# Seven block products in place of a plain output product for the first two token blocks, and quads of whole weights

## The chip, the cores and the metric

The kernel runs on one core of one Trainium2 chip. TensorE (PE) multiplies matrices into PSUM, VectorE (DVE), ScalarE (ACT) and GpSimd (POOL) work on elements, SyncE (SP) issues most transfers. The metric is the device time of one execution in microseconds, the median of three runs.

## The reference, cut to what matters

Three layers in float32: a chunked attention, a gated layer and a layer with a rational activation. The change is in the gated layer (its output product) and in the attention's softmax.

```python
# attention: 4 batches, 8 heads, 768 positions, head size 64, chunks of 32 queries,
# each against 8 memory keys and a window of 56 keys: 64 keys a chunk
a = exp(scores - max(scores));  a = a / (sum(a) + 1e-9);  out = a @ v_full
# gated layer: 3072 tokens, 512 -> 1536 -> 512
x = (sigmoid(x @ w_gate) * (x @ w_val)) @ w_out
# third layer: 512 -> 2048 -> 512
h = x @ w_in
P = a[0] + a[1]*h + a[2]*h**2 + a[3]*h**3
Q = 1 + abs(b[0])*abs(h) + abs(b[1])*h**2
y = (P / (Q + 1e-6)) @ w_out2
```

## The kernel before

**Products.** Each float32 operand is split into a rounded part (`hi`, written by ScalarE) and a remainder (`lo`, by VectorE), and each product is three matmuls (`TERMS`: hi·hi, hi·lo, lo·hi) of 128x128 weights on 512 tokens. Weights come as 64-bit words; `conv_scale` (two ScalarE instructions) and `conv_bits` (one on VectorE) turn 512 columns of them into float32.

**Blocks.** The 3072 tokens are six blocks of 512. Blocks 0 and 1 go through 24 steps `(j, f)`, one for each block j and each of twelve weight slices f of 128 inner columns. A step multiplies gate and value (`gate_val`, 24 matmuls into tiles `h`), forms sigmoid times value, splits it (`g_split`) and runs the output product of the step before (`out1`, 12 matmuls into four banks `acc`). Attention tiles for later blocks (`attn_*` for one tile of 128 tokens, `pair_*` for two), weight conversion, and combinations of weights for later are laid between, by step number, with `at(step, function, ...)`.

**Block products.** Blocks 2 to 5 are taken as two pairs. For a pair of blocks `ja, ja + 1` and a pair of slices `fp`, gate and value are seven products of sums and differences of block operands (`PRODUCTS`, function `quad`), each of 12 matmuls, run as two halves `m` (gate, value) of 6 matmuls a product. Weights of kind "a" are loaded already split (`wqa`, 512 KB), those of kind "s" (sums, `wqs`, 256 KB) are loaded whole and split. The result is held in tiles `gh` by names "11", "21", "12", "22" (slice even or odd, first or second block). The output product of a pair is then seven block products too (`OUTS`), over three groups k of four slices: 21 visits `(i, k)` of 12 matmuls (`out_step`, or `early` for the three that lie among the quads). Before a visit its operand is formed by differences (`o_pre`), split (`o_split`, 1024 wide, tiles `oh` and `ol`) and its weights are loaded (`o_weights`).

**Third layer.** Blocks 0 to 5 in three pairs, by products `q_X`, `q_Y`, `q_Z` and an output product into `acc`; the text of this part is not touched.

**Order.** All operations are recorded, and a planner (`Recorder.plan`) orders them before they are issued. TensorE keeps the order of recording. For the others it simulates the engines with estimated costs, takes the task with the earliest due time (`late`), and not much earlier than that (`window`), if the buffers that it needs are free. Each engine then runs its list in order, waiting on semaphores. Every recorded instruction has line L485, so tiles tell them apart; a tile's name is that of the buffer's last naming.

**Buffers.** Pools `w` (20 of 4 KB a partition), `x` (4) and `b` (8) of 8 KB, `g` (4), `t` (7, used as 14 halves), and PSUM pools `acc` (4 banks) and `ps` (4 banks).

Of the kernel before, what the change touches and what calls it, by code (L numbers as in the profile page):

```python
# [11 lines left out]
F32 = mybir.dt.float32  # L12
# [30 lines left out]
AHEAD = 3  # L43
# [148 lines left out]
class Recorder:  # L192
# [13 lines left out]
    def cost(self, t, op, args, kw):  # L206
# [107 lines left out]
    ORDERED = "gwxb"  # L314
    DMA_WINDOW, CAP, DMA_CAP, STORE_CAP, RATE = 12.0, 12.0, 12.0, 14.0, 350e3

    def plan(self):
# [45 lines left out]
        events = []  # L363
        self.stalls = []
        while left:
# [3 lines left out]
            for e in engines:  # L369
# [46 lines left out]
                used = now if t.table else used  # L416
                if t.table and t.table != table:
                    table, extra = t.table, 1.29
# [70 lines left out]
def fused_kernel(ctx: ExitStack, tc: tile.TileContext, q, k, v, w1, w2, coef, x2d, w2o, wq2, wqa, wqs, wqo, out):  # L489
# [100 lines left out]
    BYSET = (1, 3)  # L590

# [25 lines left out]
    def attn_exp(t):  # L617
        s = s_sb[t]
        if t not in BYSET:
# [3 lines left out]
        r = rs[t] = spool.tile([P, NSET, 1], F32, tag="r", name=f"r{t}")  # L623
        sps = sc_ps.pop(t, None)
        for h in range(2):
            for i in range(4):
# [63 lines left out]

    def pair_qk(t):
# [19 lines left out]

    def pair_max(t):
# [4 lines left out]
        if edge(t) or edge(t + 1):  # L717
# [4 lines left out]
            else:  # L722
# [5 lines left out]
        mv = m.rearrange("p (a h) w -> p a h w", h=2)  # L728
        for h in range(2):
# [76 lines left out]
    def unit1(f, u):  # L806
        if u == 2:
            if ("o", f) not in wf:
                wf["o", f] = t2(f"wfo{f}")
            return wf["o", f]  # L810
# [26 lines left out]
    def split_out_hi(key, src):  # L837
        t = split_tile(key)
        nc.scalar.activation(out=halves(t, 0), in_=src.rearrange("p (m c) -> p m c", m=2), func=ACTF.Copy)

# [1385 lines left out]
```

## Time and profile before

| | |
|---|---|
| median of three runs | 1119.76 us (1119.12 to 1121.26) |
| the profiled execution | 1118.92 us |
| its span in the trace | 1117.1 us |
| TensorE busy | 1104.8 us, 99% of the span |
| VectorE busy | 954.3 us, 85% |
| ScalarE busy | 777.7 us, 70% |
| transfers | 303.05 MB |

The span runs from the first to the last profiled instruction; the time of an execution also holds what lies around it. Busy times are unions of instructions; as instructions overlap, one instruction's own duration is longer than the time it adds.

### The profile page before, as it was taken

The page shows a single profiled execution, that of the slowest core. Times are in us where ns is not written, and L with a number is a line of the kernel's source. Part 1 is how long each engine was busy: PE and PEld are TensorE (multiplying, and loading weights), DVE is VectorE, ACT ScalarE, POOL GpSimd, SP SyncE. Part 2 cuts the span into 40 slices and gives each one's busy share as a digit, 9 for nine tenths or more (in the row PEclk, how much of TensorE's full clock was granted, in tenths as well). Part 3 has the DMA queues.
Part 4 walks back from the last instruction along what each step waited for, and adds up shares of the span by engine and source line. Part 5 has one row for each costly group of instructions (what it writes and reads, how often), then busy time and mean ns, then how long its engine had stood idle before and what let it go on. Part 6 is the DMA issues. An engine that isn't in the chain of part 4 may idle for free.

```text
span 1117.1 us, 20117 instructions
## 1 busy us (share of the span) xinstructions
PE 1104.8 (99%) x7743; PEld 905.7 (81%) x7743; DVE 954.3 (85%) x1284; ACT 777.7 (70%) x1159; POOL 23.1 (2%) x39
## 2 busy tenths in 40 slices
PE   8999999999999999999999999999999999999998
PEld 4888888888888788888878888888888887888887
DVE  4798868887899898799889799999889989999992
ACT  5999555665566675565375798875898874998952
POOL 0000000000000000000000000000000000000000
PEclk8999999999999999999999999999999999999999
DMA  9899869988877887798948687789577888687682
GB/s 369 311 352 363 317 243 385 324 306 308 310 243 275 307 309 247 276 367 309 329 146 294 191 268 206 226 292 318 170 234 211 235 295 292 197 255 207 219 248 93
DMA packets 111167, 303.05 MB, mean 271 GB/s; under 512 B 10848, under 2 KB 11104, under 8 KB 111072
## 3 DMA queue, kind: packets, MB, share of 16 engines
q1 hardware_dynamic: 107040, 287.78, 73.6%
q0 software_dynamic: 3456, 12.58, 6.2%
q8 instruction: 61, 1.00, 0.4%
q10 hardware_dynamic: 576, 1.41, 0.3%
q14 instruction: 34, 0.28, 0.1%
HBM read 225.18 MB, written 63.96 MB: 259 GB/s over the span
## 4 chain that ended last, share of the span: by engine, by line
PE 84%; issue 12%; DVE 1%; DMA 1%; ACT 1%; POOL 0%; POOLq 0%; ACTq 0%
PE acc L485 22%; PE p L485 19%; PE h L485 12%; PE q_X L485 9%; PE ob_X L485 6%; PE q_Z L485 4%; PE ob_Z L485 3%; PE xp L485 2%; PE q_Y L485 2%; PE sp L485 2%; PE ob_Y L485 2%; PE tp L485 1%; DMA q<-u 1%; PE idle L485 1%; DMA k<-k_in 0%
## 5 line engine op out<-in xcount | busy, mean ns | idle before, releaser
L485 PE MATMUL acc<-w2o,G 128*128 128x512 f32 x1152 | 268.4, 389 | 0.0
L485 PEld LDWEIGHTS acc<-w2o,G 128*128 128x128 f32 x1152 | 216.2, 188 | 44.9
L485 PE MATMUL q_X<-x,wi 128*128 128x512 f32 x576 | 146.4, 389 | 0.7 <-ACT hA L485 0.7
L485 PE MATMUL p<-b,wpq_s 128*128 128x512 f32 x576 | 138.6, 389 | 0.0
L485 PE MATMUL h<-x,wp 128*128 128x512 f32 x576 | 137.5, 392 | 0.0
L485 PEld LDWEIGHTS q_X<-x,wi 128*128 128x128 f32 x576 | 108.0, 188 | 23.7 <-ACT hA L485 1.1
L485 PEld LDWEIGHTS p<-b,wpq_s 128*128 128x128 f32 x576 | 108.0, 188 | 22.7 <-issue 0.3
L485 PEld LDWEIGHTS h<-x,wp 128*128 128x128 f32 x576 | 107.4, 188 | 22.4
L485 ACT ACTIVATE st<-st 128x512 f32<-128x512 f32 (+1 forms) x124 | 77.1, 667 | 8.5 <-DMA st<-w_in 8.4
L485 PE MATMUL p<-x,wpq_a 128*128 128x512 f32 x288 | 73.6, 391 | 0.0
L485 PE MATMUL q_Z<-x,wi 128*128 128x512 f32 x288 | 73.1, 389 | 0.0
L485 PE MATMUL acc<-g,wp 128*128 128x512 f32 x288 | 72.1, 394 | 0.0
L485 PEld LDWEIGHTS q_Z<-x,wi 128*128 128x128 f32 x288 | 54.1, 188 | 11.2
L485 PEld LDWEIGHTS p<-x,wpq_a 128*128 128x128 f32 x288 | 53.7, 188 | 11.4
L485 PE MATMUL ob_X<-oh,ow 128*128 128x512 f32 x192 | 62.3, 392 | 0.3 <-ACT oh L485 0.3
L485 PEld LDWEIGHTS acc<-g,wp 128*128 128x128 f32 x288 | 53.1, 188 | 11.5
L485 ACT ACTIVATE u<-q,qc 128x1024 f32<-128x1024 f32 x48 | 54.9, 1146 | 10.3 <-DMA q<-u 9.4
L485 DVE SCALAR_TENSOR_TENSOR q<-q,u 128x1024 f32<-128x1024 f32 x48 | 58.2, 1219 | 4.1 <-ACT u L485 4.1
L485 DVE SCALAR_TENSOR_TENSOR t<-t,cf,u 128x1024 f32<-128x1024 f32 x48 | 61.2, 1278 | 0.0
L485 ACT ACTIVATE u<-u 128x1024 f32<-128x1024 f32 (+1 forms) x57 | 55.9, 988 | 5.4 <-DVE u L485 4.9
L485 ACT ACTIVATE hb<-q_X 128x512 f32<-128x512 f32 x48 | 28.4, 591 | 38.6 <-PE q_X L485 38.5
L485 ACT ACTIVATE G<-hb 128x512 fp32r<-128x512 f32 x48 | 29.9, 626 | 31.4 <-PE acc L485 27.7
(355 smaller groups left out, 2007.5 us busy)
## 6 DMA issues: line engine op xcount, KB each, us to landing
w2o<-w2o SPq DMA_DIRECT2D x96, 512.0 KB, 4.9
wi<-wq SPq DMA_DIRECT2D x72, 512.0 KB, 4.8
st<-w_in SPq DMA_DIRECT2D x62, 512.0 KB, 6.2
ow<-wqo SPq DMA_DIRECT2D x42, 512.0 KB, 6.2
wpq_a<-wqa SPq DMA_DIRECT2D x36, 512.0 KB, 5.9
v<-v_in SPq DMA_DIRECT2D x24, 512.0 KB, 5.7
wpq_s<-wqs SPq DMA_DIRECT2D x48, 256.0 KB, 5.8
q<-u POOLq DMA_DIRECT2D x24, 512.0 KB, 6.0
```

Source lines behind the costliest of these rows:

```text
L485: getattr(getattr(self.nc, t.eng), op)(*[real(x) for x in args], **{n: real(x) for n, x in kw.items()})
```

## The change

- The output product of blocks 0 and 1 is no longer made step by step (`out1`, `g_split`, `store1` go). Sigmoid times value of all 24 steps is held in `gh` tiles, and the product is made as seven block products like that of the other pairs: six visits (i of 0 and 1) in steps 14 to 23 with weights that stay in SBUF (`"o1"`, `"o2"`), and 15 visits after the steps (`outs(0, O0, STEPS0)`).
- Output weights are loaded and converted apart (`load_wo`, `conv_wo`) from step 8 on; the sums of gate and value weights (`w_comb`) come from step 3 on in place of step 10.
- The gate and value weights that the quads read are stored and loaded whole (256 KB), and split after the load.
- A quad takes both halves m of a product before the next product, in another order of products, over banks X and Y of two halves each. Loads run five products ahead.
- The softmaxes of pairs 8, 10, 12 and 14 are taken set by set: exponential with the maximum as bias and a running sum, for each of 16 sets of 64 keys. Pair 20 is copied out of PSUM first.
- Pairs 8 to 14, eight second-layer weights and the combinations of tokens move to other steps; the planner lets stores to DRAM go up to 30 us ahead, and holds a change of activation table back only while tasks of the loaded table remain.

```diff
-AHEAD = 3
+AHEAD = 5
...
-            t.window = self.DMA_WINDOW
+            t.window = self.STORE_WINDOW if out.cell.row == 1 << 60 else self.DMA_WINDOW
...
+    STORE_WINDOW = 30.0
...
-                        if t.table and table and t.table != table and now > used + 1.5 and t.late > now - stall + 4:
+                        if t.table and tables.get(table) and t.table != table and now > used + 1.5 and t.late > now - stall + 4:
...
+    SETS = (8, 10, 12, 14)
...
-        if t not in BYSET:
+        if t not in BYSET + SETS:
...
-        r = rs[t] = spool.tile([P, NSET, 1], F32, tag="r", name=f"r{t}")
+        n = NSET if t < NPAIR else 2 * NSET
+        r = rs[t] = spool.tile([P, n, 1], F32, tag="r", name=f"r{t}")
...
+    COPIED = (20,)
...
+        if t in SETS:
+            for h in range(2):
+                nc.vector.tensor_reduce(out=mv[:, :, h, 0], in_=sps[h], axis=AX.X, op=ALU.max)
+            sc_ps[t] = sps
+            set_shift(t, m)
...
-        r = spool.tile([P, 2 * NSET, 1], F32, tag="r", name=f"r{t}")
-        nc.vector.tensor_reduce(out=r[:, :, 0], in_=s, axis=AX.X, op=ALU.add)
+        if t not in SETS:
+            r = rs[t] = spool.tile([P, 2 * NSET, 1], F32, tag="r", name=f"r{t}")
+            nc.vector.tensor_reduce(out=r[:, :, 0], in_=s, axis=AX.X, op=ALU.add)
+        r = rs.pop(t)
...
-        tiles = [None] * 3
+        tiles = [None] * 2
         if 0 < f < 3:
-            pair = [bpool.tile([P, 2, 512], I64, tag="b", name=f"stp{f}_{i}") for i in range(2)]
-            tiles = [pair[0][:, 0], pair[0][:, 1], pair[1][:, 0]]
-        for u in range(3):
+            pair = bpool.tile([P, 2, 512], I64, tag="b", name=f"stp{f}")
+            tiles = [pair[:, 0], pair[:, 1]]
+        for u in range(2):
             load_stage(f"1_{f}_{u}", w1[:, f, u * 512 : (u + 1) * 512], tiles[u])
...
+    def load_wo(f):
+        load_stage(f"o_{f}", w1[:, f, 1024:1536])
+
+    def conv_wo(f):
+        conv_scale(f"o_{f}")
+        t = so[f] = t2(f"so{f}")
+        conv_bits(f"o_{f}", t)
...
-            nc.vector.tensor_tensor(out=sg, in0=sg, in1=pt, op=ALU.mult)
+            o = f"{1 + f % 2}{1 + j}"
+            nc.vector.tensor_tensor(out=g_held(0, o, f // 2), in0=sgs.pop((j, f)), in1=pt, op=ALU.mult)
...
-        (("a", 0, 0), "11", 0),
-        (("s", 1), "2", 1),
-        (("s", 0), "1", 2),
-        (("s", 2), "3", 3),
-        (("a", 0, 1), "21", 0),
-        (("s", 3), "22", 2),
-        (("a", 1, 1), "4", 3),
+        (("a", 0, 0), "11", "X"),
+        (("a", 0, 1), "21", "Y"),
+        (("s", 1), "2", "X"),
+        (("s", 2), "3", "Y"),
+        (("s", 0), "1", "X"),
+        (("a", 1, 1), "4", "Y"),
+        (("s", 3), "22", "X"),
...
-            key = quad_key(ja, fp, w)
-            if w[0] == "a":
-                load_split(key, wqa[2 * fp + w[1], w[2]])
-                continue
-            t = split_tile(key)
+            t = split_tile(quad_key(ja, fp, w))
             hi, lo = t[:, 0], t[:, 1]
-            nc.sync.dma_start(out=lo.bitcast(F32), in_=wqs[4 * fp + w[1]])
+            src = wqa[fp, w[1] + w[2]] if w[0] == "a" else wqs[4 * fp + w[1]]
...
-    def quad(ja, fp, m, fill):
+    def quad(ja, fp, visit):
...
+            if i < 2:
+                for m in range(2):
+                    bank[n, m] = ps(f"p{ja}_{fp}_{m}_{n}")
+            wt, x = wp.pop(quad_key(ja, fp, w)), xop[ja, o]
+            for m in range(2):
+                for kt in range(2):
+                    c = m * 256 + kt * P
+                    for t, (a, b) in enumerate(TERMS):
+                        nc.tensor.matmul(
+                            bank[n, m],
+                            lhsT=wt[:, a, c : c + P],
+                            rhs=x[:, kt, b],
+                            start=(i in (0, 1, 3) and kt == 0 and t == 0),
+                            stop=(kt == 1 and t == 2),
+                            skip_group_check=True,
+                        )
+            if i + AHEAD < len(PRODUCTS):
+                quad_load(ja, fp, i + AHEAD, 1)
+            elif fp < NF1 // 2 - 1:
+                quad_load(ja, fp + 1, i + AHEAD - len(PRODUCTS), 1)
+
+        def copy(name, n):
+            t = [t2(f"{name}_{ja}_{fp}_{m}") for m in range(2)]
+            for m in range(2):
+                nc.scalar.activation(out=t[m], in_=bank[n, m], func=ACTF.Copy)
+            return t
+
+        def add(t, n):
+            for m in range(2):
+                nc.vector.tensor_tensor(out=t[m], in0=t[m], in1=bank[n, m], op=ALU.add)
 
...
+            if c is None:
+                sg, y = t2(f"sg{j}_{f}"), bank["X", 1]
+                nc.scalar.activation(out=sg, in_=bank["X", 0], func=ACTF.Sigmoid)
+            else:
+                sg, y = c
+                nc.scalar.activation(out=sg, in_=sg, func=ACTF.Sigmoid)
...
         product(0)
-        u = t2(f"u_{tag}")
-        nc.scalar.activation(out=u, in_=bank[0], func=ACTF.Copy)
+        h = copy("h", "X")
         product(1)
-        add(u, u, bank[1])
+        add(h, "Y")
+        done(ja, f0, h)
         product(2)
-        v = t2(f"v_{tag}")
-        add(v, u, bank[2])
+        u = copy("u", "X")
+        visit()
         product(3)
-        add(v, v, bank[3])
-        done(jb, f1, v)
+        z = copy("z", "Y")
         product(4)
-        done(ja, f0, None)
-        fill()
+        add(z, "X")
+        done(jb, f1, z)
         product(5)
-        c12 = t2(f"c12_{tag}")
-        add(c12, u, bank[2])
-        done(jb, f0, c12)
+        add(u, "Y")
+        done(ja, f1, u)
         product(6)
-        add(u, u, bank[3])
-        done(ja, f1, u)
+        done(jb, f0, None)
...
-    HELD_B = {2: ("12", "11"), 4: ()}
+    HELD_B = {0: ("11", "21"), 2: (), 4: ()}
...
-    def out1(j, f, mid=None):
...
+        if ja == 0 and i < 2:
+            ow[ja, i, k] = [flat(wp[f"o{1 + i}", 2 * k + f])[:, 0:512] for f in range(2)]
+            return
...
+    def early(ja, i, k):
+        o_weights(ja, i, k)
+        o_split(ja, i, k)
+        o_mm(ja, i, k)
...
+    def w1_store(fp):
+        t = wf["gv", fp]
+        nc.sync.dma_start(out=wqa[fp, 0:2].rearrange("u p n -> p u n"), in_=t[:, 0])
+        nc.sync.dma_start(out=wqa[fp, 2], in_=t[:, 1, 1])
...
+    def o_split1(fp):
+        split_out(("o1", fp), so[2 * fp], 1)
+        split_out(("o2", fp), so[2 * fp + 1])
...
+    def o_store1(fp):
+        nc.sync.dma_start(out=wqo[fp, 0], in_=flat(wp["o1", fp])[:, 0:512].bitcast(F32))
+        store_split(("o2", fp), out_slots(fp, 2))
...
-        s0 = 10 + i // 2
+        s0 = 2 * (i // 4) + 3 + i % 4 // 2
...
+    for fp in range(NF1 // 2):
+        s0 = 8 + 2 * fp
+        for f in (2 * fp, 2 * fp + 1):
+            at(s0, load_wo, f)
+            at(s0 + 1, conv_wo, f)
+        at(s0 + 1, o_split1, fp)
+        at(s0 + 2, o_store1, fp)
+        at(s0 + 2, o_comb, fp)
+        at(s0 + 3, o_store, fp)
+    EARLY0 = ((14, 0, 0), (16, 1, 0), (18, 0, 1), (19, 1, 1), (21, 0, 2), (23, 1, 2))
+    for si, i, n in EARLY0:
+        at(si, early, 0, i, n)
+    for n in range(3):
+        at(max(EARLY0[2 * n][0] + 1, 12 + 4 * n + 3), o_pre, 0, n, "13")
+    STEPS0 = [(i, n) for i in range(2, len(OUTS)) for n in range(NF1 // 4)]
...
-    for t, s0, s1 in ((8, 9, 14), (10, 12, 17), (12, 15, 20), (14, 18, 22)):
+    O0 = len(steps)
+    S1 = O0 + len(STEPS0)
+    for t, s0, s1 in ((8, 13, 18), (10, 16, 21), (12, 19, O0 + 1), (14, 22, O0 + 5)):
...
+    combs(2, [(O0 + i, o, 0) for i, o in zip((2, 3, 5, 8, 10), ("1", "2", "3", "22", "4"))])
+    combs(2, [(O0 + i, o, 1) for i, o in zip((6, 7, 8, 10, 12), ("1", "2", "3", "22", "4"))])
+    at(S1 - 3, quad_load, 2, 0, 0, AHEAD)
...
-    conv_out = [4, 5, 7, 17, 19, 20, 22, S1] + [S1 + i for i in range(5, 12)] + [Q2 + 8]
+    conv_out = [S1, S1 + 1, S1 + 2, S1 + 3] + [S1 + i for i in range(5, 12)] + [O1 + i for i in (6, 9, 12, 15)] + [Q2 + 8]
...
-            g_split((1, j, f), sgs.pop((j, f)), 512)
             run(attn_qk, attn_max, conv2_hi, conv2, x_comb_hi)
-            run(o_whole, o_comb)
-            if si:
-                out1(*steps[si - 1], mid=lambda: run(pair_out, pair_qk, pair_max))
+            run(conv_wo, o_split1, o_comb)
+            run(pair_out, pair_qk, pair_max)
             run(pair_sum)
+            run(o_pre)
+            run(early)
             run(x_comb_lo, conv2_lo, conv2_bits, comb2)
             run(done2)
 
...
+        outs(0, O0, STEPS0)
...
-            wqa = dp.tile([NF1, 2, P, 2, 512], F32, name="wqa")
+            wqa = dp.tile([NF1 // 2, 3, P, 512], F32, name="wqa")
```

Edits left out here: the names of the moved calls in the step loop and in `quads` (which now calls `quad` once per pair of slices, with the second half's side work in `visit`), the first weights' conversions at the start, where those of the output weights go, and the deleted bodies of `out1`, `g_split`, `store1` and `o_whole`.

## Rows read from the trace of the kernel before

**Rows 1.** The page: busy us of each engine, and TensorE's clock in 40 slices.

```profile
PE 1104.8 (99%) x7743; PEld 905.7 (81%) x7743; DVE 954.3 (85%) x1284; ACT 777.7 (70%) x1159; POOL 23.1 (2%) x39
...
PEclk8999999999999999999999999999999999999999
```

**Rows 2.** Chain that ended last: start us, us, what.

```profile
41.50 2.72 PE acc L485 x12
44.22 5.44 PE h L485 x24
...
424.53 8.16 PE ob_X L485 x36
...
449.01 57.12 PE p L485 x252
```

**Rows 3.** TensorE's timeline at both ends of quads: start us, us, instruction, idle before.

```profile
388.38 0.50 PE L485 MATMUL ob_X<-ol,ow 128*128 128x512 f32 x1 [1.18 <-DVE ol L485]
...
571.67 0.49 PE L485 MATMUL ob_X<-oh,ow 128*128 128x512 f32 x1 [0.25 <-ACT oh L485]
573.17 0.50 PE L485 MATMUL ob_X<-ol,ow 128*128 128x512 f32 x1 [1.01 <-DVE ol L485]
```

**Rows 4.** Windows: length, busy us of PE, PEld, DVE, ACT, POOL, then clock, DMA share, GB/s.

```profile
40.00:60.00 20.00, 20.00 (x209) 16.14 (x208) 17.45 (x30) 19.97 (x37) 0.00 (x0) 1.00 0.93 313
...
30.62:138.55 107.93, 107.93 (x1077) 87.91 (x1077) 90.64 (x160) 94.67 (x169) 0.34 (x2) 1.00 0.95 337
138.55:254.09 115.54, 115.54 (x1361) 95.69 (x1361) 90.11 (x152) 67.17 (x113) 0.34 (x2) 1.00 0.86 314
254.09:387.20 133.11, 133.11 (x1073) 109.37 (x1072) 114.62 (x171) 77.34 (x121) 0.49 (x3) 1.00 0.82 292
388.38:449.01 60.63, 60.63 (x752) 50.63 (x753) 51.22 (x64) 40.18 (x62) 0.00 (x0) 1.00 0.76 261
...
573.17:606.18 33.01, 33.00 (x144) 27.03 (x145) 32.44 (x44) 23.46 (x33) 0.00 (x0) 1.00 0.77 254
```

**Rows 5.** Groups of instructions, shapes apart, TensorE: busy us, mean ns of one.

```profile
L485 PE MATMUL acc<-g,wp 128*128 128x512 f32 x288 | 72.1, 394 | 0.0
```

**Rows 6.** VectorE's timeline near 386 us.

```profile
385.37 0.69 DVE L485 TENSOR_TENSOR gh<-v,c 128x512 f32<-128x512 f32 x1
385.98 1.22 DVE L485 TENSOR_TENSOR ot<-gh,gh 128x1024 f32<-128x1024 f32 x1
387.11 1.22 DVE L485 TENSOR_TENSOR ol<-gh,oh 128x1024 fp32r<-128x1024 f32 x1
```

**Rows 7.** ScalarE's timeline near 388 us.

```profile
387.54 0.63 ACT L485 ACTIVATE wpw<-c 128x512 fp32r<-128x512 f32 x1
388.06 1.78 ACT L485 ACTIVATE st<-st 128x512 int32<-128x512 uint32 x3
```

**Rows 8.** Groups of instructions, shapes apart, ScalarE.

```profile
L485 ACT ACT_TABLE_LOAD x25 | 32.1, 1283 | 10.6 <-DMA wqs<-sf 5.7 <-PE h L485 2.2 <-issue 2.2
...
L485 ACT ACTIVATE s<-s 128x1024 f32<-128x1024 f32 x8 | 8.5, 1061 | 0.1
```

**Rows 9.** ScalarE's timeline in a softmax taken set by set.

```profile
10.44 0.31 ACT L485 ACTIVATE s<-sp,m 128x64 f32<-128x64 f32 x1
10.64 0.20 ACT L485 ACTIVATION_READ_ACCUMULATOR s<-sp,m 128x1 f32 x1
10.73 0.32 ACT L485 ACTIVATE s<-sp,m 128x64 f32<-128x64 f32 x1
```

**Rows 10.** Transfers by issue: count, KB each, median us to landing.

```profile
wpq_a<-wqa SPq DMA_DIRECT2D x36, 512.0 KB, 5.9
```

**Rows 11.** Waits of SyncE's queue: us in total, times, longest.

```profile
SPq L485 <- PE acc L485: 108.6, 43, 9.1
```

**Rows 12.** TensorE's timeline at the start.

```profile
27.07 0.54 PE L485 MATMUL xp<-at,v 64*64 64x32 f32 x22 [0.49 <-issue]
...
30.27 3.98 PE L485 MATMUL h<-x,wp 128*128 128x512 f32 x16
```

More of the change, by code (lines that the diff above doesn't have):

```diff
@@ L362, in plan @@
         order, ends, half, now, stall, left = [], [], None, 0.0, 0.0, len(tasks)
-        events = []
+        events, tables = [], {}
+        for t in tasks:
+            if t.table:
+                tables[t.table] = tables.get(t.table, 0) + 1
         self.stalls = []
@@ L416, in plan @@
                 used = now if t.table else used
+                if t.table:
+                    tables[t.table] -= 1
                 if t.table and t.table != table:
@@ L710, in pair_qk, with set_shift @@
         sc_ps[t] = sps
+    def set_shift(t, m):
+        nc.vector.tensor_scalar(out=m, in0=m, scalar1=-1.0 / float(D) ** 0.5, scalar2=None, op0=ALU.mult)
+        nms[t] = m
     def pair_max(t):
@@ L835, in halves, with split_out @@
         return t.rearrange("p m (b c) -> p m b c", b=2)[:, :, b]
-    def split_out_hi(key, src):
+    def split_out(key, src, m=2):
         t = split_tile(key)
-        nc.scalar.activation(out=halves(t, 0), in_=src.rearrange("p (m c) -> p m c", m=2), func=ACTF.Copy)
-    def split_out_lo(key, src):
-        hi, lo = (halves(wp[key], b) for b in range(2))
-        src = src.rearrange("p (m c) -> p m c", m=2)
+        src = src.rearrange("p (m c) -> p m c", m=2)[:, 0:m]
+        hi, lo = (halves(t, b)[:, 0:m] for b in range(2))
+        nc.scalar.activation(out=hi, in_=src, func=ACTF.Copy)
         nc.vector.tensor_tensor(out=lo, in0=src, in1=hi.bitcast(F32), op=ALU.subtract)
@@ L1113, in o_weights @@
     def o_weights(ja, i, k):
-        t = ow[ja, i, k] = wpool.tile([P, 2, 512], F32R, tag="w", name=f"ow{ja}_{i}_{k}")
+        if ja == 0 and i < 2:
+            ow[ja, i, k] = [flat(wp[f"o{1 + i}", 2 * k + f])[:, 0:512] for f in range(2)]
+            return
+        t = wpool.tile([P, 2, 512], F32R, tag="w", name=f"ow{ja}_{i}_{k}")
+        ow[ja, i, k] = [t[:, f] for f in range(2)]
         nc.sync.dma_start(out=t.bitcast(F32), in_=wqo[2 * k : 2 * k + 2, OUTS[i][1]].rearrange("f p n -> p f n"))
@@ L1250, in pv @@
             xt[j] = [
-                b_tile(f"x{j}_{h}", F32R, [P, 2, 2, 512]) if j >= 4 else x_tile(f"x{j}_{h}") for h in range(2)
+                b_tile(f"x{j}_{h}", F32R, [P, 2, 2, 512]) if j >= 2 else x_tile(f"x{j}_{h}") for h in range(2)
             ]
@@ L1268, in scale1 @@
     def scale1(f):
-        for u in range(3):
+        for u in range(2):
             conv_scale(f"1_{f}_{u}")
     def bits1(f):
-        for u in range(3):
+        for u in range(2):
             conv_bits(f"1_{f}_{u}", unit1(f, u))
@@ L1373, in at @@
         plan.setdefault(si, []).append(call)
-    GV, OUT, ALL = (0, 1), (2,), (0, 1, 2)
+    GV = (0, 1)
     for si, (j, f) in enumerate(steps):
         if si:
-            at(si - 1, w1_hi, j, f, GV if j else ALL)
-            at(si - 1, w1_lo, j, f, GV if j else ALL)
-        early = 1 if f % 2 else 0
-        if j == 0:
-            at(si, w1_store, j, f, OUT + ((early,) if f >= 8 else ()))
-        else:
-            at(si, w1_store, j, f, [u for u in ((1,) if f % 2 else GV) if f < 8 or u != early])
-            at(si - 1, w1_load, j, f, OUT)
+            at(si - 1, w1_hi, j, f, GV)
+            at(si - 1, w1_lo, j, f, GV)
+        if j and f % 2 == 0:
+            at(si, w1_store, f // 2)
         if si and j == 0:
@@ L1591, in fused_kernel @@
             run(*LOADS)
-            run(w1_load, quad_load)
+            run(quad_load)
             run(*STORES)
@@ L1609, in fused_kernel, with begin, end, visit @@
         EARLY_AT = dict(zip((5, 6, 9), EARLY))
-        def early(ja, i, k):
-            o_weights(ja, i, k)
-            o_split(ja, i, k)
-            o_pre(ja, k, "13" if i == 0 else "24x")
-            o_mm(ja, i, k)
         def quads(ja, s0):
-            for i in range(NF1):
-                fp, m = divmod(i, 2)
+            def begin(i):
                 run = runner(s0 + i)
                 store1_end()
-                if m == 0 and fp < NF1 // 2 - 1:
-                    quad_load(ja, fp + 1, 0, AHEAD)
                 run(*STORES)
                 run(*LOADS)
-                quad(ja, fp, m, lambda: run(attn_exp, conv2_hi, conv2_lo, conv2))
+                run(attn_exp, conv2_hi, conv2_lo, conv2)
+            def end(i):
+                run = runner(s0 + i)
                 run(conv2_bits, comb2, pair_sum)
                 run(done2)
-                if (ja, i) == (2, 0):
-                    out1(*steps[-1])
                 if i in EARLY_AT:
-                    early(ja, *EARLY_AT[i])
+                    i, k = EARLY_AT[i]
+                    early(ja, i, k)
+                    o_pre(ja, k, "13" if i == 0 else "24x")
                 run(pair_qk, pair_max)
                 run(pair_t)
+            for fp in range(NF1 // 2):
+                def visit():
+                    end(2 * fp)
+                    begin(2 * fp + 1)
+                begin(2 * fp)
+                quad(ja, fp, visit)
+                end(2 * fp + 1)
         def out_step(ja, i, k):
```

128 lines of the change are left out of this document (22 added, 106 removed).

## Prediction

> **What bounds the kernel now.** [...] A busy share of matmuls can hide slack, so next comes the chain that ended last: from 30.6 us on it is a row of matmul stretches that touch each other, with 12 matmuls of 512 columns taking 2.72 us, 24 taking 5.44 us, and 252 in a row 57.12 us [rows 2]. So one such matmul costs 2.72 / 12 = 0.2267 us of the end time, and TensorE's queue is the path. Then the gaps on that path, by TensorE's timeline: past the start there are two that a reader should see, 1.18 us at 387 and 0.25 + 1.01 = 1.26 us at 571, both at the first output visit after a run of quads, which waits for the rounded and the remainder part of its operand [rows 3]. Last the windows by stage: VectorE and ScalarE are nearly as full as TensorE in places, so a shorter TensorE stage may hand the bound to them [rows 4].
>
> The sum is made against the profiled execution: 1118.92 us, that is 1117.1 of span and 1.8 around it. The median of the runs shown, 1119.76, lies 0.84 above it; I add that at the end.
>
> **Matmuls removed.** The output product of blocks 0 and 1 was 24 steps of 12 matmuls, the 288 of [rows 5]. As seven block products over three groups of four weight slices it is 21 visits of 12, so 252. Saved: 36 x 0.2267 = 8.16 us. Gate and value of blocks 0 and 1 keep their 24 per step; the joined quads keep 7 x 12 = 84 per weight pair, as two halves of 42 before. The attention's and the idle matmuls stay.
>
> [...]
>
> **The two gaps.** They come from the order inside the last quad: the operand "11" of weight slices 8 to 11 is finished after the fifth of seven products, so 2 x 1.36 = 2.72 us (and at 387 some transposes) before its first use, while product, rounding (1024 wide, about 1.0) and remainder (1.13) [rows 6] need more. With the new order "11" is finished after the second product; five more follow, 5 x 2.72 = 13.6 us. What is late next: "21" of the same slices, made after the sixth product, used two visits after the quad, 2.72 + 5.44 = 8.2 us later, against two adds (0.6 each), sigmoid (about 0.5), product (0.6), rounding (1.0), remainder (1.13), in all 4.4. It holds. Saved: 1.18 + 1.26 = 2.44 us; bounds 0 and 2.44, and I take 2.44, because the chain is cut by more than ten us.
>
> **Is there still cover in block 0's steps?** TensorE's twelve steps shrink: the window of 107.93 us [rows 4] is 12 x 5.44 of gate and value, 11 x 2.72 of output, and 12.7 of attention; without the output it is 78. Costs per instruction go by pitch, since durations overlap: ScalarE 0.52 for a 512-wide copy, (1.78 - 0.67) / 2 = 0.555 for a conversion half [rows 7]; VectorE 0.6 for 512, 1.13 for 1024 wide [rows 6].
> ScalarE before: 12 x (6 x 0.555 + 3 x 0.52 + sigmoid 0.52 + rounding 0.52) = 71.2, three second-layer weights 4.9, so 18.6 of the 94.67 are attention and table loads. After: 12 x (4 x 0.555 + 2 x 0.52 + 0.52) = 45.4, the same 18.6, four output slices 4.4 and one pair's splits 2.0: 70.4 of 78, 90% (before 88%).
> VectorE before: 12 x 8 x 0.6 = 57.6, three second-layer weights 3.6, four weight combinations 2.4, so 27.0 of the 90.64 are attention. After: 12 x 5 x 0.6 = 36, up to 18 combinations 10.8, 27.0 less four 1024-wide operations of pair 8, which comes four steps later (4.5), output slices 6.2: 75.5 of 78. That is 97%, but the combinations and output slices, 17 us, are not used before step 14, so only 58.5 of 78 is due. The stretch from 40 to 60 us with ScalarE at 19.97 of 20, and the visits from 573 to 606 with VectorE at 32.44 of 33.01, show that such loads can lie behind TensorE without a gap [rows 4]. I cost it at nothing; without that cover, rival 1.
>
> **Block 1's steps.** TensorE: 115.54 less 12 output steps plus six early visits, 99 us. VectorE: 90.11, less 51 (remainders of the gated product 7.2, whole output weights 7.2, combinations 12, token combinations 10.8, second-layer weights 4.8, softmax subtract and sum of four pairs 8 x 1.13 = 9.0), plus 26 (eight conversions 4.8, splits 5 + 6.8, differences 6.8, rest), plus at most 17 left over: 65 to 82. The softmaxes set by set cost ScalarE: one 1024-wide exponential of about 1.0 [rows 8] becomes sixteen at a pitch of 10.73 - 10.44 = 0.29 [rows 9], so +3.6 a pair, 14.6 for four. With eight conversions (8.9), early splits (5.8), output splits (4.6) and what leaves (20), ScalarE goes from 67.17 to about 82 of 99. Covered. The more relaxed table rule in the planner moves a few loads of 1.28 us [rows 8], on ScalarE only.
>
> **New output visits, 15 x 2.72 = 40.8 plus two pairs' attention, about 47 us.** VectorE: 15 remainders 17, six differences 6.8, four adds 2.4, 18 on token combinations 10.8, five weight remainders 3.0, rest 1.4: 41. The same visits of blocks 2 and 3 ran at 51.22 of 60.63 without a gap [rows 4]. Two seams are new (steps to visits, visits to quads). The trace has no such seam; bounds are 0 and, for each, the 1.2 that a seam of quads to visits cost [rows 3]. The first visit there takes slices 0 to 3, long finished, so I stay near the lower end, at a quarter of 2 x 1.2: +0.6.
>
> **Quads of blocks 2 to 5.** Per weight pair ScalarE gets three roundings of plain weights (1.56) and four more copies (2.0), VectorE three remainders more and four adds fewer. Blocks 2 and 3 also take three second-layer weights more: ScalarE 77.34 + 21 + 5 = 103, VectorE 114.62 - 3.6 + 3.6, of about 133 us [rows 4]. A bank is again rewritten 4.08 us after its last matmul. The plain loads are half the size of the 36 split ones (512 KB, 5.9 us to land) [rows 10] and start five products ahead, 13.6 us; rounding and remainder (1.1) still fit. Cost: nothing.
>
> **Queues and start.** By the code, transfers shrink: split weights 24 x 0.52 MB written and 36 x 0.52 read become 18 x 0.26 and 36 x 0.26; output weights are no longer reloaded by step, but 15 visits read 0.52 MB. 303 becomes about 286 MB, all on SyncE's queue. Stores may be issued up to 30 us ahead; one that waits for its data holds the loads behind it, as SyncE does now (108.6 us on one group alone) [rows 11] without TensorE waiting. In the start three loads fewer lie in front; but TensorE goes from attention to the first gate matmul at 30.27 with one wait of 0.49 us [rows 12], so at most that is to be had. I take 0.
>
> **Sum.** 1118.92 - 8.16 - 2.44 + 0.6 = 1108.9; against the median, 1109.8 us.
>
> **Rivals.**
> 1. VectorE or ScalarE becomes the bound in block 0's steps. For it: 97% and 90% by my count, and in-order engines; one combination ahead of an urgent remainder delays it by 0.6 us, and 24 of them share the stretch. Against: only 58.5 of 78 us is urgent, and block 1's steps have room. At its worst the whole 17 us comes first while 19.5 us are idle; 3 to 8 us of it, gives 1112.5 to 1118. Chance 0.15.
> 2. The joined quads wait at their seams: the last product's X banks are read by sigmoid and product when the next visit wants banks, and all four PSUM buffers are in use. Twelve visits at 0.5 to 0.9 us (a sigmoid, or a product and its latency) give 6 to 11 us, 1116 to 1121. Against: the Y banks are free by then, and the sigmoid can run under the second half of the product. Chance 0.08.
> 3. Slower: SBUF slots run out. The split output weights stay in the 20-buffer pool from step 9 until their early visit, by the code six to eight buffers, while each step wants two stage tiles and two split tiles in 5.44 us in place of 8.16. A load lands about 6 us after issue and needs some 4 us of conversion, so with less than two steps of lead every step waits. The gain is gone from 10 / 24 = 0.42 us a step; at 0.6 the 24 steps lose 14.4 and the time is 1123.6. Against: the third unit of every step no longer needs its tile, nor do the rereads of block 1, and the steps that still load gate and value weights end where the pinning begins. Chance 0.10. [...]
> 4. The removed matmuls are worth less than their pitch. [...] Chance 0.02.
>
> **How the numbers follow.** My case has 0.65 and reaches from 1107.5 (no seam, the 0.49 of the start, and the 0.64 by which the fastest run shown lies under the median give 1108.1; the rest is for what three loads fewer may do to the start) to 1112.5 (both seams at 1.2, and 0.9 of small waits). Rival 1 is faster by over 0.2% with 0.12 of its 0.15, rival 2 with half of its 0.08; the rest of both lies within 0.2% (2.2 us, about what a measurement can tell from no change). Faster: 0.65 + 0.12 + 0.04 + 0.02 = 0.83; same 0.03 + 0.04 = 0.07; slower 0.10. The range for 8 in 10 leaves out rival 3 and most of rival 2: 1107.5 to 1116.5.
>
> **What would show it.** Right: 36 matmuls fewer, no wait at the first output visit after either run of quads, matmul stretches of 5.44 us touching each other from about 30 us on, VectorE's total near 955 and ScalarE's near 845 us, some 286 MB moved. Wrong: gaps in the first 80 us after the start with VectorE or ScalarE full (rival 1), a gap of equal size every 19 us in the quads (rival 2), or TensorE waiting on weights whose loads were issued late (rival 3); the clock falling after such gaps would add to each.

## The result, and the profile after

Measured: 1108.95 us (median of four runs, 1107.99 to 1109.27) against 1120.11 of the kernel before in the same comparison (1119.12 to 1121.26): a ratio of 0.9899, 95% interval 0.9881 to 0.9916, so 11.2 us or 1.0% faster. Forecast were 1109.8 us and a range of 1107.5 to 1116.5. The profiled execution took 1108.83, its span is 1107.0, 10.1 less than before.

The page of the changed kernel: busy time of each engine, TensorE's clock in 40 slices, all transfers, and the queue of instructions (packets, MB, share of 16 engines), of which the last section speaks.

```profile
PE 1093.4 (99%) x7700; PEld 899.1 (81%) x7707; DVE 957.3 (86%) x1267; ACT 848.0 (77%) x1366; POOL 23.1 (2%) x39
...
PEclk8999999999999999999999999999999999999999
...
DMA packets 111121, 288.91 MB, mean 261 GB/s; under 512 B 10800, under 2 KB 11056, under 8 KB 111024
...
q8 instruction: 61, 1.00, 0.4%
```

Against [rows 1], weight loads fell from 7743 to 7707: 36 fewer, as the change says (the matmul column lacks seven idle matmuls that left no record). VectorE's total hardly moved and ScalarE's rose by 70, to 957 and 848, where 955 and 845 were forecast. Transfers are 288.91 MB, where some 286 were forecast.

The chain that ended last, where [rows 2] stood: start us, us, what.

```profile
30.86 16.35 PE h L491 x72
48.00 5.71 PE h L491 x24
54.50 11.14 PE h L491 x48
...
249.46 2.72 PE p_X L491 x12
252.18 2.72 PE p_Y L491 x12
254.90 2.72 PE p_X L491 x12
```

It is still TensorE's queue. In the joined quads the products alternate between banks X and Y, and each piece of 2.72 us begins where the last one ends.

TensorE's timeline at the two places of [rows 3], the first output visit after each run of quads:

```profile
375.82 2.66 PE L491 MATMUL p_X<-b,wpq_s 128*128 128x512 f32 x11
378.32 1.03 PE L491 MATMUL tp<-ident,s 128*128 128x128 f32 x8
379.11 0.48 PE L491 MATMUL ob_X<-oh,ow 128*128 128x512 f32 x1
379.42 0.40 PE L491 MATMUL ob_X<-ol,ow 128*128 128x512 f32 x1
...
560.81 1.98 PE L491 MATMUL p_X<-b,wpq_s 128*128 128x512 f32 x8
562.62 0.39 PE L491 MATMUL ob_X<-oh,ow 128*128 128x512 f32 x1
562.85 0.39 PE L491 MATMUL ob_X<-ol,ow 128*128 128x512 f32 x1
```

No bracket stands behind the first `oh` and `ol`, so both are there when TensorE arrives.

Windows by stage, with the columns of [rows 4]: block 0's steps, block 1's, the new output visits, quads of blocks 2 and 3, their visits, quads of blocks 4 and 5, the first visits of their output, and the rest, mostly the third layer.

```profile
30.51:107.06 76.55, 76.55 (x818) 61.96 (x817) 70.45 (x132) 68.56 (x124) 0.34 (x2) 1.00 0.85 292
107.06:202.41 95.35, 95.02 (x1147) 78.33 (x1146) 77.65 (x123) 76.55 (x205) 0.34 (x2) 1.00 0.86 306
202.41:249.46 47.05, 47.05 (x453) 39.20 (x453) 37.97 (x50) 32.09 (x64) 0.00 (x0) 1.00 0.62 203
249.46:379.10 129.64, 129.64 (x1061) 106.93 (x1060) 112.71 (x165) 103.47 (x169) 0.49 (x3) 1.00 0.83 287
379.35:440.38 61.03, 60.76 (x754) 50.56 (x753) 54.03 (x68) 46.76 (x75) 0.00 (x0) 1.00 0.85 298
440.38:562.78 122.40, 122.40 (x542) 101.39 (x541) 107.98 (x170) 89.82 (x158) 0.00 (x0) 1.00 0.82 282
562.78:595.42 32.64, 32.64 (x146) 27.04 (x145) 31.36 (x39) 22.07 (x32) 0.00 (x0) 1.00 0.76 250
595.42:1107.00 511.58, 506.24 (x2233) 418.60 (x2231) 449.79 (x485) 391.79 (x490) 21.00 (x24) 1.00 0.73 232
```

The second column is the length, the third TensorE's busy time: up to 595 they differ only by 0.33 and 0.27. VectorE has 92% of block 0's steps and 96% of the visits from 562.78 on, and TensorE waits in neither.

TensorE's waits: us in total, times, longest.

```profile
PE q_X L491 <- ACT hb L491: 1.3, 1, 1.3
PE idle L491 <- issue: 1.2, 7, 0.2
PE sp L491 <- issue: 1.0, 3, 0.5
PE xp L491 <- issue: 0.4, 1, 0.4
PE ob_Z L491 <- issue: 0.3, 1, 0.3
```

The 0.33 and 0.27 of the windows are "issue" waits, in which the profile shows nothing waited for.

### The profile page after: what moved, and what is told of

It reads as the page before. It is cut to its first block, busy times and chain, and to the rows that moved or that the text cites. A ratio compares the mean times of both kernels' runs of the same rounds, so it can differ in the third digit from the quotient of the medians.

```text
span 1107.0 us, 20180 instructions
## 1 busy us (share of the span) xinstructions
PE 1093.4 (99%) x7700; PEld 899.1 (81%) x7707; DVE 957.3 (86%) x1267; ACT 848.0 (77%) x1366; POOL 23.1 (2%) x39
## 2 busy tenths in 40 slices
DMA packets 111121, 288.91 MB, mean 261 GB/s; under 512 B 10800, under 2 KB 11056, under 8 KB 111024
## 3 DMA queue, kind: packets, MB, share of 16 engines
q10 hardware_dynamic: 576, 1.41, 0.3%
## 4 chain that ended last, share of the span: by engine, by line
PE 96%; issue 1%; DMA 1%; ACT 0%; DVE 0%; ACTq 0%; POOLq 0%
PE acc L491 23%; PE h L491 12%; PE p_X L491 12%; PE q_X L491 11%; PE ob_X L491 9%; PE p_Y L491 9%; PE q_Z L491 6%; PE ob_Z L491 4%; PE q_Y L491 3%; PE xp L491 2%; PE ob_Y L491 2%; PE sp L491 2%; PE tp L491 1%; DMA q<-u 1%; PE idle L491 1%
## 5 line engine op out<-in xcount | busy, mean ns | idle before, releaser
L491 PE MATMUL p_X<-b,wpq_s 128*128 128x512 f32 x432 | 103.8, 389 | 0.0
L491 PEld LDWEIGHTS p_X<-b,wpq_s 128*128 128x128 f32 x432 | 81.1, 188 | 16.8
L491 PE MATMUL ob_X<-oh,ow 128*128 128x512 f32 x264 | 85.5, 392 | 0.0
L491 DVE TENSOR_TENSOR ol<-gh,oh 128x1024 fp32r<-128x1024 f32 x54 | 65.4, 1219 | 7.7 <-DMA w2o<-wpw 2.7
L491 ACT ACTIVATE st<-st 128x512 f32<-128x512 f32 (+1 forms) x104 | 66.0, 667 | 5.8 <-DMA st<-w_in 5.8
L491 ACT ACTIVATE oh<-gh 128x1024 fp32r<-128x1024 f32 x54 | 56.6, 1067 | 11.4 <-PE ob_X L491 7.9
L491 PEld LDWEIGHTS q_Z<-x,wi 128*128 128x128 f32 x288 | 54.1, 188 | 11.2
L491 PEld LDWEIGHTS ob_X<-oh,ow 128*128 128x128 f32 x264 | 49.6, 188 | 10.3
L491 PE MATMUL ob_X<-ol,ow 128*128 128x512 f32 x132 | 51.4, 389 | 0.0
```

What stands on the lines that cost most here:

```text
L491: getattr(getattr(self.nc, t.eng), op)(*[real(x) for x in args], **{n: real(x) for n, x in kw.items()})
```

## The experiments

Twelve kernels ran, in three groups of four, each group beside its own runs of the kernel before. Ratios are to those runs; their medians were 1121.03, 1121.66 and 1121.44. The groups ran on three chips, so between groups the ratios are the fairer comparison.

### The two gaps: another visit first

The kernel before, where the first visit after the quads takes an operand that is ready earlier:

```diff
-    STEPS = [(0, 2), (1, 1), (1, 2)] + ...
+    STEPS = [(1, 1), (0, 2), (1, 2)] + ...
```

> The kernel before, with one edit: after a run of quads the first output visit is (1, 1), whose operand was finished long ago, and the visit (0, 2), whose operand "11" comes out of the last quad, is second. Theory (the 2.44 us of gaps came from that operand being finished late): both waits of TensorE on oh and ol go, and the time falls by about 2.4 us, to 1117.6. Rival (a run of quads leaves VectorE so far behind that any first visit waits): a wait of about 1 us stays at each of the two places and the time is within 0.5 us of before.

Measured: 1119.80, ratio 0.9982 (0.9970 to 0.9994), 1.2 us less where 2.4 were expected. TensorE's timeline of this run at the end of the first and of the second run of quads:

```profile
388.98 0.40 PE L485 MATMUL ob_Y<-ol,ow 128*128 128x512 f32 x1
...
572.11 0.39 PE L485 MATMUL ob_Y<-oh,ow 128*128 128x512 f32 x1
572.34 0.39 PE L485 MATMUL ob_Y<-ol,ow 128*128 128x512 f32 x1
...
577.99 0.49 PE L485 MATMUL ob_Y<-oh,ow 128*128 128x512 f32 x1 [0.28 <-ACT oh L485]
579.77 0.50 PE L485 MATMUL ob_Y<-ol,ow 128*128 128x512 f32 x1 [1.28 <-DVE ol L485]
```

The first visit no longer waits at either place: the gaps of [rows 3] came from a late operand, as the prediction said. At 388 the wait is gone; at 572 it moved to visit (1, 2), whose operand "21" is now the late one. So the order of visits alone is worth about one gap. The new product order, which finishes both operands earlier, took both.

### What 36 matmuls are worth

The kernel before with 36 matmuls of its plain output product left out:

```diff
             for i, (a, b) in enumerate(TERMS):
+                if i == 1 and 0 < f < 10 and j * NF1 + f < 23 and d >= 2:
+                    continue
```

> The kernel before, without 36 of the 288 output matmuls of blocks 0 and 1 (for nine slices of block 0 or 1 the product of the rounded weights with the remainder is left out for two of the four banks, so x loses that small part). Nothing else changes. Theory (TensorE's queue is the path and one matmul of 512 columns costs 0.2267 us): 8.2 us less, 1111.9. [...] Rival (ScalarE sets the pace of block 0's steps): less than 4 us.

Measured: 1116.12, ratio 0.9947 (0.9928 to 0.9966), 4.9 us less. The chain of this run:

```profile
63.23 5.44 PE h L485 x24
68.67 2.27 PE acc L485 x10
70.94 5.44 PE h L485 x24
```

Ten take 2.27 where twelve took 2.72 [rows 2]: 0.227 each, 8.16 for 36, and neighbours touch. From the first gate matmul of a step to that of the next, 17 of the 18 edited steps are 0.41 to 0.46 us shorter than before and one is 0.12 shorter, 7.7 us in all (worked out from the starts in both traces). So the pitch stands, although the median fell by 4.9 us only. TensorE's timeline later on shows where the rest went:

```profile
411.79 1.15 PE L485 MATMUL xp<-at,v 64*64 64x32 f32 x63
415.15 0.42 PE L485 MATMUL xp<-at,v 64*64 64x32 f32 x2 [2.21 <-issue]
415.50 0.79 PE L485 MATMUL ob_Z<-oh,ow 128*128 128x512 f32 x1
416.09 0.63 PE L485 MATMUL ob_Z<-ol,ow 128*128 128x512 f32 x1
416.52 1.05 PE L485 MATMUL ob_Z<-oh,ow 128*128 128x512 f32 x2
```

A wait of 2.21 us that the kernel before does not have in its profile, and then matmul pairs of 1.05 us instead of 0.62: the granted clock, 0.77 in 412.8 to 416 us, is 0.86 and 0.97 in the two halves of 400 to 440 us, together 3.4 us of clock lost, 3.1 of it after the wait. The first gate matmul also came 1.0 us later than before, after a stop of 1.57 us in the start. Less 8.16, plus 1.0, 2.2 and 3.1, makes -1.9; this execution's span, 1115.5, is 1.6 below 1117.1. The other five executions have no trace, so for their median the same cause is likely but not shown. The last section comes back to this wait.

### The old quads in the changed kernel

Old quad function and order of products, in halves m, three loads ahead; the whole weights in DRAM stay.

```diff
-    def quad(ja, fp, visit):
+    def quad(ja, fp, m, fill):
...
-AHEAD = 5
+AHEAD = 3
```

> The changed kernel, with the quads as before: two halves of 42 matmuls, the old order of products and banks, loads three ahead. The plain weights and all else stay. Theory (joining the quads is worth the two gaps and nothing else): the waits on oh and ol come back, 1 to 2.5 us slower than the changed kernel, 1110 to 1111.5. Rival (joining is also what lets ScalarE and VectorE keep up with the plain weights): gaps within the quads, over 4 us slower. Rival (the joined quads cost something at their seams): faster than the changed kernel.

Measured: 1114.54, ratio 0.9934 (0.9915 to 0.9953): by medians 5.6 above the changed kernel's 1108.95, by ratios (0.9899 and, when it ran again, 0.9881) 4 to 6. TensorE's waits, and two windows within the quads:

```profile
PE q_X L491 <- ACT hA L491: 2.7, 1, 2.7
...
PE ob_X L491 <- DVE ol L491: 1.2, 2, 0.7
PE p L491 <- DVE u L491: 1.1, 1, 1.1
...
PE p L491 <- DVE c L491: 0.8, 1, 0.8
```

```profile
320.00:340.00 20.00, 18.86 (x205) 15.15 (x204) 20.00 (x28) 14.30 (x22) 0.20 (x1) 1.00 0.81 279
340.00:360.00 20.00, 19.20 (x84) 15.29 (x83) 20.00 (x32) 12.64 (x19) 0.00 (x0) 1.00 0.58 196
```

VectorE is busy in all 40 us, and the products wait for it. With weights split after the load and the old number of additions, VectorE (981.1 us in all, against 957.3) is the bound there; the joined quads, with four additions a pair fewer, take that load off. The old quads' own waits here make 3.1 us. The profiled execution (1117.45) is the slowest of the six. The third layer's wait of 2.7 (1.3 in the changed kernel) is in its time, with a granted clock of 0.57 in the 4 us behind it (938 to 942), and no run shows whether the quads cause that wait.

### The softmaxes

Both new treatments off (`SETS = ()`, `COPIED = ()`), and, in another group, the set-by-set softmaxes alone:

```diff
-    SETS = (8, 10, 12, 14)
+    SETS = ()
```

> The changed kernel, with the softmaxes of all pairs as before (one exponential a pair, subtract and sum on VectorE). Theory (VectorE has room in block 1's steps): within 1 us of the changed kernel, 1108 to 1110; VectorE busier by about 9 us in all, ScalarE less busy by about 14. Rival (VectorE is the bound there without it): gaps in block 1's steps or the visits after them, 3 to 9 us slower.

> The changed kernel, without the softmaxes set by set (pairs 8, 10, 12 and 14 as before), but with pair 20 still copied out of PSUM. Theory (the old softmax is as well hidden, and a little better): 1 to 3 us below the changed kernel. Rival (the copy of pair 20 was what cost): the same as the changed kernel within 1 us.

Measured: 1106.23, ratio 0.9859 (0.9834 to 0.9884), and 1108.27, ratio 0.9877 (0.9856 to 0.9897); the changed kernel again stands at 0.9881 in the second one's group, so the gain of 1 to 3 us expected there did not show (0.5 by medians). With the sets alone off, VectorE has 965.6 us instead of 957.3 and ScalarE 833.4 instead of 848.0, and behind the start no new wait appears. The work moves from one engine to the other, and neither side is on the path. The 1106.23 looks 2.7 better than 1108.95, but the intervals of the ratios just overlap, and its profile differs from the changed one by an earlier start (first gate matmul at 29.5 instead of 30.5), by the third layer's 1.3 us wait and three of the changed kernel's four "issue" waits of 0.27 us and more, which it lacks.

### The changed kernel again

> The changed kernel itself, for its time beside that of the other runs on one chip and for what varies from one execution to the next. Theory (the 2.7 us between it and the run with the old softmaxes are real): 0.988 to 0.991 of before. Rival (they are chance of start and chip): 0.986. The first gate matmul began at 30.5 us in its profile and at 29.5 in the run with the old softmaxes, although the two kernels have the same order on every engine up to there: if the start is chance, it will lie elsewhere this time.

Measured: 1108.80, ratio 0.9881 (0.9861 to 0.9900): the first comparison holds on another chip. The start did not lie elsewhere: the first gate matmul came at 30.4 again. In the other profiles of kernels made from the changed one it lies between 30.2 and 30.8, and the 29.5 stands alone; why stays open.

### How near VectorE and ScalarE are to being the bound

In each of the 23 steps after the first, two instructions of extra work on a constant, on VectorE (680 ns each, 0.6 by pitch, 27.6 us in all), and in another kernel on ScalarE (627 ns each):

```diff
         for si, (j, f) in enumerate(steps):
             run = runner(si)
+            for _ in range(2 if si else 0):
+                nc.vector.tensor_reduce(out=dum, in_=ones, axis=AX.X, op=ALU.max)
```

> The changed kernel, with two more VectorE operations of about 0.6 us (a maximum over 512 elements that nobody reads) recorded in each step but the first. That is 11 x 1.2 = 13 us more in block 0's steps, where VectorE is busy for 70.45 of 76.55 us, of which some 17 are not due there, and 14 us more in block 1's, where it is busy for 77.65 of 95.35. Theory (what is not due moves out, and the cover is real): within 2 us of the changed kernel. Rival (the steps are at VectorE's edge): block 0's steps grow by 7 us or more, 1116 or more.

> The changed kernel, with two more ScalarE copies of 512 elements (about 0.5 us each, of a tile of ones onto itself) recorded in each step but the first: 11 us more in block 0's steps, where ScalarE is busy for 68.56 of 76.55 us, and as much in block 1's, 76.55 of 95.35. Theory (ScalarE has less that may move out of block 0's steps than VectorE, so this is its edge): gaps in block 0's steps, 3 to 8 us slower. Rival (ScalarE too is covered): within 1.5 us of the changed kernel.

VectorE, measured: 1113.94, ratio 0.9938 (0.9914 to 0.9962), 5.1 slower than the changed kernel in the same group. Neither the theory (within 2 us) nor the rival (block 0's steps grow) came true. Windows of block 0's steps and of 120 to 140, the only two waits of TensorE in 128 to 168 us, and what ScalarE did before the first:

```profile
30.50:107.00 76.50, 76.50 (x818) 62.04 (x817) 69.85 (x130) 66.19 (x120) 0.36 (x2) 1.00 0.76 271
...
120.00:140.00 20.00, 17.85 (x70) 13.96 (x70) 19.83 (x39) 15.58 (x49) 0.00 (x0) 0.91 0.98 363
```

```profile
133.09 10.06 PE L491 MATMUL h<-x,wp 128*128 128x512 f32 x36 [2.06 <-ACT s L491]
...
165.16 3.03 PE L491 MATMUL h<-x,wp 128*128 128x512 f32 x12 [0.92 <-ACT sg L491]
```

```profile
129.27 1.28 ACT L491 ACT_TABLE_LOAD   x1 [1.80 <-DVE m L491]
```

Block 0's steps take the extra work without a gap: the planner lets combinations slip, and VectorE's busy time there does not even rise. The debt comes due at 120 to 140 us, where VectorE is full. There its maximum `m` comes late, ScalarE waits 1.80 us for it, and then loads a table and takes a softmax set by set out of PSUM (`sp`) before TensorE may go on. The granted clock of 0.91 in these 20 us costs another 1.8. So some slack was left, but less than 27.6 us over the steps.

ScalarE, measured: 1115.90, ratio 0.9956 (0.9939 to 0.9973). Its window of block 0's steps, and TensorE's timeline at the one large wait:

```profile
30.50:107.00 76.50, 76.50 (x817) 61.91 (x817) 68.39 (x125) 75.70 (x138) 0.34 (x2) 1.00 0.87 304
```

```profile
165.66 1.43 PE L491 MATMUL sp<-k,q 64*32 64x64 f32 x122
...
171.59 0.43 PE L491 MATMUL sp<-k,q 64*32 64x64 f32 x6 [4.50 <-issue]
171.95 0.79 PE L491 MATMUL ob_Y<-oh,wpo 128*128 128x512 f32 x1
```

ScalarE has 75.7 of 76.5 us, 99%, and TensorE does not wait for it. The time expected (3 to 8 us slower) came, but not from the gaps that were expected. The 6.8 us that this span has more lie elsewhere: 4.50 us of "issue" between the 122nd and the 123rd of 128 small matmuls, and a lower granted clock until 177.2 us (0.83 in 160 to 180 us), some 2.9 us. All seven runs have a lower mean clock (0.992 to 0.995 against 0.997), so it was probably not one execution's accident.

### Slots, planner, loads ahead, early sums

Four parts, each undone alone in the changed kernel:

```diff
-    wpool = pool("w", 20)
+    wpool = pool("w", 16)
```
```diff
-    STORE_WINDOW = 30.0
+    STORE_WINDOW = 12.0
...
-                        if t.table and tables.get(table) and t.table != table and ...
+                        if t.table and table and t.table != table and ...
```
```diff
-AHEAD = 5
+AHEAD = 3
```
```diff
-        s0 = 2 * (i // 4) + 3 + i % 4 // 2
+        s0 = 10 + i // 2
```

> The changed kernel, with 16 in place of 20 buffers in the pool of weights and operands (w). Theory (slots were not scarce with the output weights of blocks 0 and 1 kept in SBUF): up to 3 us slower. Rival 3 of the prediction (slots are what block 0's and block 1's steps live on): gaps on TensorE that recur in those steps, 10 us or more.

> The changed kernel, with the planner's two old rules: stores to DRAM at most 12 us ahead of their due time, and a change of activation table held back whenever another table was used just before. Theory (both move work of SyncE and ScalarE only, which is hidden): within 1 us of the changed kernel, 0.988 to 0.990 of before. Rival (stores that come late hold up loads behind them on SyncE's queue): TensorE waits on weights, 2 us or more slower.

> The changed kernel, with the weights of the quads loaded three products ahead in place of five: 8.2 us of lead in place of 13.6, against 5.0 us to land, 0.5 for the rounding and 0.6 for the remainder. Theory (three would do): within 1 us of the changed kernel. Rival (rounding and remainder of plain weights wait behind other work on ScalarE and VectorE, so that 2 us of slack is not enough): TensorE waits on wpq tiles in the quads, 3 us or more slower.

> The changed kernel, with the sums of gate and value weights (24 VectorE operations of 0.6 us) from step 10 on, as before the change, in place of step 3. Block 0's steps lose about 10 us of VectorE's work, block 1's gain as much: 77.65 + 10 of 95.35. Theory (this work is due late and may lie in either stage): within 1.5 us of the changed kernel. Rival (VectorE's edge is the beginning of block 1's steps, where the run with more VectorE work had its gaps): a wait of TensorE there, 3 us or more slower.

| undone | us | ratio, 95% |
|---|---|---|
| 16 buffers in pool `w` | 1112.02 | 0.9910 (0.9889 to 0.9932) |
| both planner rules | 1111.01 | 0.9905 (0.9887 to 0.9923) |
| five loads ahead (three) | 1108.39 | 0.9879 (0.9860 to 0.9897) |
| early sums (from step 10) | 1108.61 | 0.9887 (0.9868 to 0.9906) |

With four buffers fewer no gap recurs in the steps; behind the start, TensorE's largest waits in that run are `sp<-issue`, 1.4 us of it at one place, and two of 0.6 in the third layer. Its median is 3.2 us above the changed kernel's in the same group, but the intervals overlap. The planner's rules are worth some two us by medians of two groups, which is not clear of noise either, and no wait on weights shows in that profile; three loads ahead and late sums cost nothing that these runs can tell. No run here is measurably better than the changed kernel.

## Why the prediction was right, step by step

The forecast sum and what the profiles show for each term:

| term | forecast | shown |
|---|---|---|
| 36 matmuls | -8.16 | 36 weight loads fewer; 0.227 each where ten stand for twelve |
| two gaps | -2.44 | both gone, -3.24 from start to start (below); their cause confirmed by the order of visits |
| two smaller pauses of the kernel before, 346.3 and 578.5 us | not in it | gone, -0.46 from start to start |
| two new seams | +0.6 | 0: 202.41 to 249.46 is busy throughout |
| start | 0 | +0.24 (first gate matmul 30.27 to 30.51) |
| "issue" waits behind the start, 166.83 and 412.05 us | not in it | +0.90 from start to start (0.33 and 0.27 idle) |
| from the third layer's first matmul on | 0 | +0.66, nearly all in one wait (0.7 to 1.3) |

With 8.16 for the matmuls that makes -10.1, and the span fell by 10.1. The first `q_X` comes 10.8 earlier than before (windows' ends 606.18 and 595.42).

The forecast priced the gaps by idle time between records, and that was too little: a matmul's record is longer than the pitch (0.48 us below, against 0.23), so it hides part of a wait. The start-to-start figures of the table are worked out from the starts of matmuls in the two traces.

```profile
386.72 0.48 PE L485 MATMUL ob_X<-oh,ow 128*128 128x512 f32 x1
```

This is the matmul of the kernel before that stands ahead of the first one in [rows 3]. Their starts lie 1.66 us apart where a pitch is 0.23, so 1.43 was lost and not 1.18; at 571 us it was 1.81 and not 1.26. That the forecast came so close (1109.8 against 1108.95) is thus partly luck: 1.3 us more gain than was summed stands against 0.9 of "issue" waits and 0.9 of start and third layer that were not in the sum, and against seams that cost nothing.

**Cover.** The forecast of 78 us for block 0's steps came out at 76.55. ScalarE's 90% was right. VectorE's 97% was 92%: part of the early combinations slipped behind, as the text allowed. The two experiments with extra work show the cover to be real, and where it ends: at the start of block 1, not in block 0. That is where the prediction put the room: it counted 82 of 99 us as busy (76.6 and 77.7 of 95.35 measured), but a mean over twelve steps hid a stretch with VectorE at 99% once 27.6 us were added.

**Joined quads.** ScalarE 103 and VectorE 114.6 were forecast for the first run of quads, 103.5 and 112.7 measured. The step "cost: nothing" was right: joined quads with whole weights, against old quads with split ones, gain the gaps and no more. What the prediction did not ask is which of the two carries the other. With whole weights, the old quads lose 4 to 6 us, and 3.1 us of waits for VectorE stand inside and behind the quads of the profiled execution.

**Seams.** +0.6 was a quarter of a bound from [rows 3]; the first visits' operands were finished long before, and nothing was lost.

**Rivals.** Rival 1 needs less slack than there is: no gap in block 0's steps, not even with ScalarE at 99%. Rival 2: the pieces of 2.72 us touch, and no wait for a bank is listed. Rival 3: no gap recurs with 20 buffers, and none with 16. Rival 4: ten matmuls for twelve shorten a piece by 0.45 us, and 17 of 18 steps by as much.

## What to carry to other kernels

Count removed matmuls by the pitch of touching pieces in the chain of waits, and check that each engine beside TensorE has its due work covered in short stretches, not only over a stage. Where an operand is late, making it earlier removes the gap; taking another one first may only pass it on. Take what a gap costs from start to start, not from the idle time between records. After any change look for "issue" waits as well, because a few us at one place can eat a gain of this size, and more through the clock: of the 8.16 us expected, one wait of 2.21 and the 3.1 of lower clock behind it took 5.3 in the run without the 36 matmuls.

## What the hardware showed that was not expected

TensorE stops where no engine, semaphore or transfer of data is named: 0.3 to 4.5 us in these traces, always within or just behind a dense run of small attention matmuls. The page gives a clue: queue q8, of kind "instruction", moves 61 packets and 1.00 MB, so 16.4 KB each; TensorE's matmul and weight-load records, 2 x 7707, make 253 for each packet, and with its 205 semaphore and drain instructions 256. The changed kernel's four stops (13.08, 26.90, 166.83 and 412.05 us) come after 446, 956, 4282 and 9402 records of TensorE, semaphores included: steps of 510, 3326 and 5120, which are 2, 13 and 20 times 256 but for at most two records (with the seven matmuls that left no record, exactly). So the stops lie whole multiples of 256 records apart; the records from one such place to the next are called a block here, and by the count above there is one packet for each. The start times of the q8 packets in the traces, in us (worked out from their records):

```
kernel               at      stops   goes on  packet starts  from packet to go on
changed              xp      26.90    27.31       24.83         2.48
changed              sp     166.83   167.16      164.72         2.44
changed              ob_Z   412.05   412.32      409.72         2.60
changed, again       ob_Z   411.95   413.26      410.87         2.39
16 buffers           sp     166.80   168.21      165.82         2.39
visit order          xp      25.34    26.93       24.47         2.46
36 matmuls fewer     xp     412.94   415.15      412.81         2.34
work on ScalarE      sp     167.09   171.59      169.38         2.21
```

The wait varies by 4.2 us, while the time from the packet's start to the next matmul stays at 2.2 to 2.6. 128 small matmuls and their weight loads are 256 records; 122 of them took 1.43 us (from 165.66 in the run with work on ScalarE) and 126 took 2.06 (from 410.87 in the run without the 36 matmuls), less than that time. That TensorE waits there for the packet is the author's inference from these times; no record names what it waited for.

The other block boundaries fit it. The fourteen traces have 840 of them. At 42 TensorE stopped for more than 0.25 us with "issue", the 0.49 us of [rows 12] among them, and it made no such stop anywhere else. There the packet had started 2.2 to 2.6 us before TensorE went on (3.1 in one case); at the 798 crossed without a stop it had started at least 2.4 us ahead. In the changed kernel the four stops have the four shortest leads of 60, 2.4 to 2.6 us.

With the packets matched to the boundaries in order, as above, a packet starts near the moment of the boundary before its own, from 4.9 us before it to 6.4 us after it in these traces. Why one starts later than another stays open. At 167 us the packet started 0.5 us after that moment in the changed kernel and 5.2 after it with the extra work on ScalarE: 2.1 us before the stop in the one, 2.3 after it in the other. The data transfers were dense before the 2.21 us wait (a DMA share of 1.04 in the 7.8 us before it), but less so before the longest (0.74 in 160 to 165 us, 0.87 in 165 to 167), and as dense before the shortest (1.04 in 405 to 409.7 of the changed kernel), so that alone does not decide it. It was not tried to move the boundary of a block out of such a run by some instructions more or fewer ahead of it. Both long stops (2.21 and 4.50 us) also brought 6.8 us at a granted clock of 0.50, from within the stop on. The 1.41 us at 166.80 and the 1.31 at 411.95 brought none; in the start, where the granted clock had already been 0.50 a few us before (in 18.1 to 24.8 us of the changed kernel), the 1.59 of the visit-order run was followed by 3.4 us of it, and the 1.56 of the run with the sets alone off by none.
